# Attention and token/channel mixer on one core: the passage between two pairs of chunks, and the second weights' sums, issued in another order

## The chip, the core and the metric

The kernel runs on one core of a Trainium2 chip. The metric is the device time of one execution in microseconds (us). Of three executions of the kernel before, the median is 850.93 us (849.22 to 851.91).

The core's engines are called as in the profile: PE (TensorE, matrix products into the PSUM banks; PEld is its weight load), DVE (VectorE), ACT (ScalarE), POOL (GpSimd) and SP (SyncE, which here only issues DMAs). Each engine works through its own instructions in the order in which the program issues them, and waits on semaphores for the others.

## The reference

```python
def _attn_ref(q, k, v):                      # B, H, S, D = 8, 8, 576, 64; causal window of 64
    ...
    return np.matmul(attn, v)
def _moe_ref(x, w_tok1, w_tok2, w_ch1, w_ch2):   # x: (8, 576, 512)
    xt = x.transpose(0, 2, 1)
    h = np.maximum(xt @ w_tok1, 0.0) @ w_tok2
    u = x + h.transpose(0, 2, 1)
    h2 = np.maximum(u @ w_ch1, 0.0) @ w_ch2      # 512 -> 1536 -> 512
    return u + h2
```

Windowed attention gives x; a small network over the tokens gives u; a two-layer network over the channels (w_ch1, w_ch2) is added to u. Everything is fp32. The change lies wholly in the last step, the channel network.

## The kernel before

**Numbers in two parts.** Each operand is kept as a high part (a copy in the type fp32r, made by ACT, "hi") and a low part (source minus high part, a two-input subtraction on DVE or POOL, "lo"), and each product is three matmuls: hi·hi, hi·lo, lo·hi. Making the two parts of a 128x512 block is called a split.

**Stages.** The attention and the token network fill the span's first 300 us; they leave u, transposed, in DRAM (`u_dram`) as nine chunks of 512 tokens. The channel network then runs chunk by chunk. Chunks 0, 1 and 2 are done plainly: `gemm1` (12 blocks of hidden units, ft 0 to 11, of 12 matmuls each, whose result goes through `relu_split`: ACT makes hi, DVE lo) and `gemm2` (4 output blocks, ct 0 to 3). Chunks 1 and 2 do this in two halves of six ft's; the PE runs 72 matmuls of gemm1 and 72 of gemm2 in each half. The other six chunks are done in three pairs (q = 0, 1, 2) with Strassen's scheme: a 2x2 block product with seven products m1 to m7 in place of eight.

**What the pairs need.** (1) Sums and differences of the blocks of w_ch1 and w_ch2, split and written to DRAM as `w1s` and `w2s` while chunks 1 and 2 run. Those of w_ch2 come from `weight_steps2`: six rounds, each loading a piece `w2t`, making m5, m7, m6 and m3 (DVE adds, ACT copies hi into `w2p`, DVE subtracts lo) and storing them; a round takes five calls of `next(steps2)`. `w2p` has one buffer, so the hi copy of a round waits for the same store of the round before. `quarter_steps2` stores, unchanged, the blocks that m1, m2 and m4 use (w2hi, w2lo to `w2s`), in six steps. (2) For each pair the split operands of its seven products, for two halves t of the contraction: `load_raw(q, t)` loads four blocks r11, r12, r22, r21 of u, `sums` makes t1, r12, t2 on DVE, `sum4` one more, and `prep(q, m, t)` splits the source of product m. `part="hi"` and `part="lo"` do one half of a split; the lo goes to DVE unless an engine is given.

**A pair** runs `pair_f` six times (f = 0 to 5, 7 products of 6 matmuls each, and evictions out of PSUM) and, after every second f, `pair_op` (the second layer, a group, t = 0 and 1, 84 matmuls). `pair_f` with even f and `pair_op`'s t = 0 share four PSUM banks, odd f and t = 1 the other four. In `pair_op`, m4 adds onto the bank of m7 and m3 onto that of m5 (`INTO`), so m4's matmuls wait until m7's result has been read out by DVE (`evict`, line 1070), and m3's until m5's has. m2 adds onto m1's bank in the same way, after an `evict` at line 1082. `combine(1)` makes the second f's operands between these evictions on DVE.

**The passage.** In a pair's third group (`more` is true) `pair_op` also prepares the next pair: the splits of t = 0, `load_raw(q + 1, 1)`, sums and splits of t = 1, all in the same queues of DVE, ACT and POOL as the group's own work. At its end POOL does six `add_common`s (line 1070, on POOL) with their stores. There are two passages, from q = 0 to 1 and from 1 to 2. The next pair's f = 0 begins with the first half (t = 0) of its products m1, m6, m7 and m5, whose operands are the first to be ready.

Of the kernel before, what the change touches and what calls it, by code (L numbers as in the profile page):

```python
# [10 lines left out]
F32 = mybir.dt.float32  # L11
# [19 lines left out]
NCT = C // P  # L31
# [24 lines left out]
NH = NFT // 2  # L56
PRODUCTS = ("m1", "m6", "m7", "m5", "m2", "m4", "m3")
# [50 lines left out]
def mixer_kernel(ctx: ExitStack, tc: tile.TileContext, qh, kh, vh, wt1, wt2, wc1, wc2, out):  # L108
# [479 lines left out]
    with ExitStack() as bctx:  # L588
# [238 lines left out]
        def load_w1(n):  # L827

            if n < (NCHUNK - N_PLAIN) // 2 * NH:
                o = n % NSLOT * SLOT  # L830
                for k, w in enumerate((w1hi, w1lo)):
                    nc.sync.dma_start(w[:, o:o + SLOT].bitcast(F32),
                                      w1s[k][:, n % NH].rearrange("p m t c -> p (m t c)"))
# [4 lines left out]
        comb, raws = {}, {}  # L838

        def load_raw(q, t):  # L840
            raws.clear()
            for name, j, ct in (("r11", 0, t), ("r12", 1, t), ("r22", 1, 2 + t), ("r21", 0, 2 + t)):
                raws[name] = px[0].tile([P, CHUNK], F32, name=f"{name}_{q}_{t}", tag=name, bufs=1)
                nc.sync.dma_start(raws[name], u_dram[pairs[q][j]][:, ct])
            for name in ("t1", "t2"):
                raws[name] = px[0].tile([P, CHUNK], F32, name=f"{name}_{q}_{t}", tag=name, bufs=1)
# [6 lines left out]
            nc.vector.tensor_sub(r["t2"], r["r22"], r["t1"])  # L853

        def sum4():
            nc.vector.tensor_sub(raws["r11"], raws["r21"], raws["t2"])

        SOURCE = {"m1": "r11", "m6": "t2", "m7": "r12", "m5": "t1", "m2": "r21", "m4": "r11", "m3": "r22"}

        def prep(q, m, t, eng=None, part=None):  # L860
            if (q, m) not in comb:
# [10 lines left out]
        for j in range(1, N_PLAIN):  # L872
            u, last = ul.pop(j), j == N_PLAIN - 1
            if last:
                tctx.close()
                px.append(bctx.enter_context(tc.tile_pool(name="px", bufs=1, reuse_waits="tile")))
                load_raw(0, 0)
            for half in range(2):
                g = []
                for ft in range(half * NH, (half + 1) * NH):  # L880
                    g.append(new_g(f"{j}_{ft}"))
                    gemm1(j, ft, u, g[-1])
                    if j == 1:
                        next(steps, None)
                        if ft == 3:
                            ul[j + 1] = load_u(j + 1, pu)
                        if ft >= NFT - 2:
                            split_u(ul[j + 1], (2 * (ft - NFT) + 4, 2 * (ft - NFT) + 5))
                            next(steps2, None)
                    elif half == 0:  # L890
                        next(steps3, None)
                        for _ in range(2):
                            next(steps2, None)
                    else:
                        if ft == 6:
                            load_w1(0)
                        if ft == 8:
                            sums()
                        for m in {8: ("m1", "m6"), 9: ("m7", "m5"), 10: ("m2",)}.get(ft, ()):
                            prep(0, m, 1)  # L900
                        if ft == 11:
                            sum4()
                if last and half == 1:
                    for m in ("m4", "m3"):
                        prep(0, m, 1)
                    load_raw(0, 0)
                    load_w1(1)
                for ct in range(NCT):
                    op = new_op(f"{j}_{half}", ct)
                    gemm2(op, ct, range(half * NH, (half + 1) * NH), g, True, True)  # L910
                    add_out(j, u[0], ct, op, half == 1)
                    if j == 1 and half == 0:
                        for _ in range(1 if ct == NCT - 1 else 2):
                            next(steps, None)
                    elif j == 1:
                        for _ in range(4):
                            next(steps2, None)
                    elif half == 0:
                        if ct == 0:
                            for _ in steps2:  # L920
                                pass
                            sums()
                        for m in (("m1", "m6"), ("m2",), ("m7",), ("m5",))[ct]:
                            prep(0, m, 0)
                        if ct == NCT - 1:
                            load_raw(0, 1)
                    else:
                        if ct in (0, 1):
                            load_w2s(ct)
                        if ct == 1:  # L930
                            sums(False)
                            sum4()
                            for m in ("m4", "m3"):
                                prep(0, m, 0)
# [20 lines left out]

        common = whole[6:]

        MADE = {**SOURCE, "m4": "t1"}

        def parts_hi(fi, m):  # L960
            nc.scalar.copy(ops_g[fi][m][0], made[MADE[m]])  # L961

        def parts_lo(fi, m, eng):
            hi, lo = ops_g[fi][m]
            eng.tensor_sub(lo, made[MADE[m]], hi.bitcast(F32))  # L965

        def combine(fi):

# [18 lines left out]
            yield  # L987
            parts_lo(fi, "m4", nc.vector)

        def pair_f(q, f, rest):  # L990

            bank, fi = banks(f"gp{q}_{f}", f % 2), f % 2
            x1, later = x1s[fi], []
            o = (q * NH + f) % NSLOT * SLOT

            def block(name, src, m, eng):
                nc.scalar.activation(made[name], src, AF.Relu)  # L997
# [4 lines left out]
                    elif eng is not None:  # L1002
                        parts_lo(fi, m, eng)

            def product(m, ts, first):
                n, b, c = PRODUCTS.index(m), bank[INTO[m]], comb[q, m]
                for k, t in enumerate(ts):
                    at = slice(o + (n * 2 + t) * P, o + (n * 2 + t + 1) * P)
                    for j, (w, h) in enumerate(((w1hi, 0), (w1hi, 1), (w1lo, 0))):
                        nc.tensor.matmul(b, w[:, at], c[:, h, t], start=(first and n < 4 and k == j == 0),  # L1010
                                         stop=(k == len(ts) - 1 and j == 2), skip_group_check=True)

            more = q + 1 < len(pairs)
            begin = q > 0 and f == 0
            next(rest, None)
            if begin:

                for m in PRODUCTS[:4]:
                    product(m, (0,), True)
            for n, m in enumerate(PRODUCTS):  # L1020
                b = bank[INTO[m]]
                if begin and n < 4:
# [32 lines left out]
        def pair_op(q, grp, ufs, more, final):  # L1055
# [50 lines left out]
            ops = combine(1)  # L1106
            if more:

                prep(q + 1, "m7", 0, part="lo")
                prep(q + 1, "m5", 0, part="lo")  # L1110
                prep(q + 1, "m2", 0, nc.gpsimd, part="lo")
            for n in range(3):
                next(ops)
            parts_lo(1, "m2", nc.vector)
# [7 lines left out]
            if more:  # L1122
                sum4()
                prep(q + 1, "m4", 0, part="hi")
                prep(q + 1, "m3", 0, part="hi")
                prep(q + 1, "m3", 0, nc.gpsimd, part="lo")
            next(ops)
            evict(0, "m2")
            if not (final and last):
# [5 lines left out]
                load_raw(q + 1, 1)  # L1135
            for t in range(2):
                end = final and last and t == 1
                for m in ("m6", "m7", "m5", "m4", "m3"):
                    product(t, m, (1,) if m in PRODUCTS[:4] else (0, 1))
                    evict(t, m)  # L1140
                    if end and m in ("m5", "m4", "m3"):
                        add_common(t, m, nc.vector)
                    if more and t == 0 and m == "m3":
                        sums()
                        for x in PRODUCTS[:4]:
                            prep(q + 1, x, 1, part="hi")
                        prep(q + 1, "m1", 1, nc.gpsimd, part="lo")
                    if more and t == 1 and m == "m6":
                        prep(q + 1, "m6", 1, part="lo")
                        prep(q + 1, "m7", 1, nc.gpsimd, part="lo")  # L1150
                        prep(q + 1, "m2", 1, part="hi")
                        prep(q + 1, "m3", 1, part="hi")
                    if more and t == 1 and m == "m7":
                        prep(q + 1, "m5", 1, part="lo")
                        sum4()
                        prep(q + 1, "m4", 1, part="hi")
                    if more and t == 1 and m == "m4":
                        prep(q + 1, "m2", 1, nc.gpsimd, part="lo")
                        prep(q + 1, "m4", 1, part="lo")
                if end:  # L1160

# [7 lines left out]
                        add_common(t, m, nc.gpsimd)  # L1169
                load_w2s((q * NGRP + grp + 1) * 2 + t)  # L1170
            if more:
                prep(q + 1, "m3", 1, part="lo")
                for t in range(2):
                    for m in ("m5", "m4", "m3"):
                        add_common(t, m, nc.gpsimd)
# [57 lines left out]
```

## Time and profile before

| | us |
|---|---|
| median of three executions | 850.93 (849.22 to 851.91) |
| the profiled execution, its own time | 850.83 |
| its span, first to last instruction | 849.0 |
| outside the span | 1.83 |
| mean granted TensorE clock | 0.986 |

The span is what the trace shows; 1.83 us of the profiled execution lie outside it. The profile's page gives for each engine its busy time, a row of digits for the span in 40 slices of 21.2 us, and the chain of work that ended last. A view by stretches gives each engine's busy time between two moments. In a timeline or a list of waits, "[0.54 <-DVE uf L1070]" reads: idle for 0.54 us before this instruction, released by the DVE instruction of line 1070 that writes `uf`. A matmul of 512 columns is listed with 0.39 us, but one starts every 0.23 us, since they overlap. "w1hi", "w2hi_r", "ghic" in the DVE and ACT rows are the buffers that hold operands during the pairs, "m" and "r" those of `prep` and `load_raw`.

### The profile page before, as it was taken

To read this page: it belongs to the slowest core of one execution; us is meant where nothing else is said; L and a number is where in the kernel's file an instruction comes from. 1 tells how busy PE (TensorE), PEld (TensorE's weight loads), DVE (VectorE), ACT (ScalarE), POOL (GpSimd) and SP (SyncE) were. 2 spreads that over 40 slices of the span, in tenths; PEclk is the share of its full clock that TensorE was granted. 3 is DMA by queue.
4 is the path that set the end of the run, shared out by engine and by line. 5 is a ranking of instruction groups with operands and counts; after the bars stand their busy time and mean duration, and the time that the engine had idled before them with its cause. 6 is when DMAs were issued, how large, how long until landed. Compare 5 with 4: busy or idle time off the path is not lost.

```text
span 849.0 us, 15802 instructions
## 1 busy us (share of the span) xinstructions
PE 806.2 (95%) x5752; PEld 658.8 (78%) x5752; DVE 627.1 (74%) x1552; ACT 423.0 (50%) x1173; POOL 182.9 (22%) x174
## 2 busy tenths in 40 slices
PE   8989999999999999999699999996999995999997
PEld 6668888888898878888488878774878784878785
DVE  5978889788855885875535667789676779676777
ACT  6978988988854422242312516072425163335150
POOL 3623444344320000000000101034401033401011
PEclk9999999999999999999799999998999999899999
DMA  9837878777545658659945957444867554755512
GB/s 356 280 130 243 262 232 291 243 253 243 179 139 165 196 179 256 204 174 295 356 155 204 359 195 268 176 174 161 290 236 261 194 197 161 282 211 206 183 72 99
DMA packets 91357, 185.90 MB, mean 219 GB/s; under 512 B 8848, under 2 KB 56336, under 8 KB 89360
## 3 DMA queue, kind: packets, MB, share of 16 engines
q1 hardware_dynamic: 89168, 183.07, 62.8%
q10 hardware_dynamic: 2112, 1.84, 0.7%
q8 instruction: 45, 0.74, 0.4%
q14 instruction: 32, 0.26, 0.1%
HBM read 140.84 MB, written 44.04 MB: 218 GB/s over the span
## 4 chain that ended last, share of the span: by engine, by line
PE 67%; DVE 16%; ACT 7%; DMA 5%; issue 3%; SPq 1%; POOL 0%; ACTq 0%; DVEq 0%
PE gp L1010 17%; PE op L1065 13%; PE op L665 10%; PE gp L656 6%; PE h L396 5%; PE up L444 5%; PE xp L348 4%; DVE uf L1070 3%; PE s L306 3%; ACT e L329 3%; PE pp L336 2%; PE up L437 2%; DVE w2lo_r L1082 2%; DMA w_dram<-w 1%; DVE gloc L965 1%
## 5 line engine op out<-in xcount | busy, mean ns | idle before, releaser
L1010 PE MATMUL gp<-m,w1hi 128*128 128x512 f32 x504 | 156.7, 393 | 0.0
L329 ACT ACTIVATE e<-e,nm 128x128 f32<-128x128 f32 x288 | 112.3, 397 | 6.3 <-DVE nm L321 6.2
L965 POOL TENSOR_TENSOR gloc<-w2hi_r,ghic 128x512 fp32r<-128x512 f32 x18 | 23.3, 1294 | 414.5 <-ACT ghic L961 405.9
L1010 PEld LDWEIGHTS gp<-m,w1hi 128*128 128x128 f32 x504 | 95.8, 190 | 20.2
L1010 PE MATMUL gp<-m,w1lo 128*128 128x512 f32 x252 | 98.6, 391 | 0.0
L1070 DVE TENSOR_TENSOR uf<-op,uf 128x512 f32<-128x512 f32 (+1 forms) x91 | 61.8, 683 | 32.9 <-PE op L1065 29.8
L1065 PE MATMUL op<-ghic,w2hi 128*128 128x512 f32 (+1 forms) x145 | 59.8, 412 | 23.5 <-DVE uf L1070 18.8
L321 DVE CUSTOM_DVE_ANT_0 e<-s,mask 128x128 f32<-128x128 f32 x288 | 65.3, 285 | 10.7 <-PE s L306 10.5
L1028 ACT COPY x<-gp 128x512 f32<-128x512 f32 x18 | 10.5, 584 | 100.7 <-PE gp L1010 100.7
L997 ACT ACTIVATE w2hi_r<-x 128x512 f32<-128x512 f32 x54 | 34.1, 632 | 48.9 <-DVE x L1034 45.1
L1065 PEld LDWEIGHTS op<-ghic,w2hi 128*128 128x128 f32 x145 | 27.4, 189 | 39.8 <-DVE uf L1070 28.5
L665 PE MATMUL op<-ghi,w2hi 128*128 128x512 f32 x128 | 51.3, 401 | 7.1 <-ACT ghi L643 7.1
L1065 PE MATMUL op<-ghic,w2lo 128*128 128x512 f32 (+1 forms) x145 | 57.2, 394 | 0.0
L1065 PE MATMUL op<-gloc,w2hi 128*128 128x512 f32 (+1 forms) x145 | 57.1, 394 | 0.0
L656 PE MATMUL gp<-ulo,w1hi 128*128 128x512 f32 x144 | 56.0, 389 | 0.0
L656 PE MATMUL gp<-uhi,w1hi 128*128 128x512 f32 x144 | 56.0, 389 | 0.0
L656 PE MATMUL gp<-uhi,w1lo 128*128 128x512 f32 x144 | 56.0, 389 | 0.0
L329 ACT ACTIVATION_READ_ACCUMULATOR e<-e,nm 128x1 f32 x288 | 56.0, 194 | 0.0
L1010 PEld LDWEIGHTS gp<-m,w1lo 128*128 128x128 f32 x252 | 47.8, 190 | 10.1
L665 PE MATMUL op<-glo,w2hi 128*128 128x512 f32 x128 | 51.3, 401 | 0.5 <-DVE glo L644 0.5
L129 POOL TENSOR_TENSOR xlo<-x,xhi 128x512 fp32r<-128x512 f32 x32 | 41.6, 1299 | 43.7 <-ACT xhi L126 43.0
L665 PE MATMUL op<-ghi,w2lo 128*128 128x512 f32 x128 | 50.7, 396 | 0.0
(165 smaller groups left out, 2013.3 us busy)
## 6 DMA issues: line engine op xcount, KB each, us to landing
v<-vh SPq DMA_DIRECT2D x36, 512.0 KB, 4.0
w1hi<-w1s SPq DMA_DIRECT2D x18, 896.0 KB, 4.9
w1lo<-w1s SPq DMA_DIRECT2D x18, 896.0 KB, 7.1
w2hi<-w2s SPq DMA_DIRECT2D x18, 896.0 KB, 4.6
w2lo<-w2s SPq DMA_DIRECT2D x18, 896.0 KB, 6.6
raw<-wc SPq DMA_DIRECT2D x32, 384.0 KB, 4.6
q<-qh SPq DMA_DIRECT2D x36, 256.0 KB, 4.6
k<-kh SPq DMA_DIRECT2D x7, 1280.0 KB, 8.0
```

Of the source, the lines that this page charges most:

```text
L129: eng_lo.tensor_sub(lo, src, hi.bitcast(F32))
L321: nc.vector.tensor_tensor_reduce(out=e[:, h], in0=s[:, h], in1=mk, scale=-scale, scalar=MAX_F32, op0=ALU.add, op1=ALU.min, accum_out=nm[:, ...
L329: nc.scalar.activation(e[:, h], e[:, h], AF.Exp, bias=nm[:, g:g + 1], scale=-1.0, accum_out=sm[:, g:g + 1])
L348: nc.tensor.matmul(xp[half * BLK:(half + 1) * BLK, h], pts[h % 2][:, h // 2, half * BLK:(half + 1) * BLK], vt[:, half, h], start=True, sto ...
L396: nc.tensor.matmul(h_ps[b][tt], w[:, o + tt * P:o + (tt + 1) * P], x, start=first and n == 0, stop=last and n == len(combos) - 1)
L444: nc.tensor.matmul(up[:, :n], hx[:, cs], w[:, tt * S + s0:tt * S + s0 + n], start=False, stop=(k == 6), skip_group_check=True)
L656: nc.tensor.matmul(gp, w[:, w1_at(ft, ct)], x[:, ct], start=(k == 0), stop=(k == 3 * NCT - 1))
L665: nc.tensor.matmul(op, w[:, at], x[:, cols], start=(first and k == 0), stop=(last and k == 3 * len(gs) - 1), skip_group_check=not (first a ...
L997: nc.scalar.activation(made[name], src, AF.Relu)
L1010: nc.tensor.matmul(b, w[:, at], c[:, h, t], start=(first and n < 4 and k == j == 0), stop=(k == len(ts) - 1 and j == 2), skip_group_check= ...
L1065: nc.tensor.matmul(bank[t][INTO[m]][:, cols], w[:, at], ops_g[fi][m][h][:, cols], start=(n < 4 and fi == j == 0), stop=(fi == fis[-1] and ...
L1070: eng.tensor_add(ufs[c][:, ct, cols], x, ufs[c][:, ct, cols])
```

## The change

1. *Order in the groups* (all nine calls of `pair_op`): the loop over the last five products runs m7, m6, m5, m4, m3 in place of m6, m7, m5, m4, m3.
2. *Splits of t = 0 in the passage*: the lo's of m7 and m5 go from DVE to POOL, and m3's hi and lo are made ahead of m2's lo; POOL has four lo's in a row there.
3. *Splits of t = 1*: m7's lo is issued directly behind m1's on POOL; the lo's of m6 and m5, the hi's of m2 and m3, `sum4` and m4 each come one product later.
4. *`sum4` writes to t1* and no longer to r11, so r11 is free for its next load earlier; `raws.clear()` at the head of `load_raw` goes.
5. *Two f's ahead*: after the passage, the first halves (t = 0) of m1, m6, m7 and m5 run for f = 0 and then for f = 1, before any second half.
6. *Chunk 2*: `steps2` gets one call per ft in half 0 (two before) and two per ct in the following gemm2 (all that was left, at ct = 0, before). The six `quarter_steps2` move from half 0 to half 1. m7's and m5's splits of t = 0 move from gemm2 to ft = 6 of half 1, with `load_raw(0, 1)` behind them; the splits of t = 1 come one ft later.

```diff
         def load_raw(q, t):
-            raws.clear()
...
         def sum4():
-            nc.vector.tensor_sub(raws["r11"], raws["r21"], raws["t2"])
+            nc.vector.tensor_sub(raws["t1"], raws["r21"], raws["t2"])
...
                     elif half == 0:
-                        next(steps3, None)
-                        for _ in range(2):
-                            next(steps2, None)
+                        next(steps2, None)
                     else:
                         if ft == 6:
+                            prep(0, "m7", 0)
+                            prep(0, "m5", 0)
+                            load_raw(0, 1)
                             load_w1(0)
-                        if ft == 8:
+                        next(steps3, None)
+                        if ft == 9:
                             sums()
-                        for m in {8: ("m1", "m6"), 9: ("m7", "m5"), 10: ("m2",)}.get(ft, ()):
+                        for m in {9: ("m1", "m6"), 10: ("m7", "m5"), 11: ("m2",)}.get(ft, ()):
                             prep(0, m, 1)
...
                         if ct == 0:
-                            for _ in steps2:
-                                pass
                             sums()
-                        for m in (("m1", "m6"), ("m2",), ("m7",), ("m5",))[ct]:
+                        for m in (("m1",), ("m6",), ("m2",), ())[ct]:
                             prep(0, m, 0)
-                        if ct == NCT - 1:
-                            load_raw(0, 1)
+                        for _ in range(2):
+                            next(steps2, None)
...
-            if begin:
-
-                for m in PRODUCTS[:4]:
-                    product(m, (0,), True)
+            if q > 0 and f == 0:
+
+                ahead.append(banks(f"gp{q}_1", 1))
+                for f1, b in enumerate((bank, ahead[0])):
+                    for m in PRODUCTS[:4]:
+                        product(m, (0,), True, f1, b)
...
-                prep(q + 1, "m7", 0, part="lo")
-                prep(q + 1, "m5", 0, part="lo")
-                prep(q + 1, "m2", 0, nc.gpsimd, part="lo")
+                prep(q + 1, "m3", 0, part="hi")
+                for m in ("m7", "m5", "m3", "m2"):
+                    prep(q + 1, m, 0, nc.gpsimd, part="lo")
...
-                for m in ("m6", "m7", "m5", "m4", "m3"):
+                for m in ("m7", "m6", "m5", "m4", "m3"):
                     product(t, m, (1,) if m in PRODUCTS[:4] else (0, 1))
                     evict(t, m)
...
-                        prep(q + 1, "m1", 1, nc.gpsimd, part="lo")
-                    if more and t == 1 and m == "m6":
+                        for x in ("m1", "m7"):
+                            prep(q + 1, x, 1, nc.gpsimd, part="lo")
+                    if more and t == 1 and m == "m5":
                         prep(q + 1, "m6", 1, part="lo")
-                        prep(q + 1, "m7", 1, nc.gpsimd, part="lo")
+                        prep(q + 1, "m5", 1, part="lo")
                         prep(q + 1, "m2", 1, part="hi")
                         prep(q + 1, "m3", 1, part="hi")
-                    if more and t == 1 and m == "m7":
-                        prep(q + 1, "m5", 1, part="lo")
+                        prep(q + 1, "m2", 1, nc.gpsimd, part="lo")
+                    if more and t == 1 and m == "m4":
                         sum4()
                         prep(q + 1, "m4", 1, part="hi")
-                    if more and t == 1 and m == "m4":
-                        prep(q + 1, "m2", 1, nc.gpsimd, part="lo")
+                    if more and t == 1 and m == "m3":
+                        prep(q + 1, "m3", 1, part="lo")
                         prep(q + 1, "m4", 1, part="lo")
```

More of the change, by code (lines that the diff above doesn't have):

```diff
@@ L855, in sum4 @@
         def sum4():
-            nc.vector.tensor_sub(raws["r11"], raws["r21"], raws["t2"])
-        SOURCE = {"m1": "r11", "m6": "t2", "m7": "r12", "m5": "t1", "m2": "r21", "m4": "r11", "m3": "r22"}
+            nc.vector.tensor_sub(raws["t1"], raws["r21"], raws["t2"])
+        SOURCE = {"m1": "r11", "m6": "t2", "m7": "r12", "m5": "t1", "m2": "r21", "m4": "t1", "m3": "r22"}
         def prep(q, m, t, eng=None, part=None):
@@ L956, in mixer_kernel @@
         common = whole[6:]
-        MADE = {**SOURCE, "m4": "t1"}
         def parts_hi(fi, m):
-            nc.scalar.copy(ops_g[fi][m][0], made[MADE[m]])
+            nc.scalar.copy(ops_g[fi][m][0], made[SOURCE[m]])
         def parts_lo(fi, m, eng):
             hi, lo = ops_g[fi][m]
-            eng.tensor_sub(lo, made[MADE[m]], hi.bitcast(F32))
+            eng.tensor_sub(lo, made[SOURCE[m]], hi.bitcast(F32))
         def combine(fi):
@@ L988, in combine @@
             parts_lo(fi, "m4", nc.vector)
+        ahead = []
         def pair_f(q, f, rest):
-            bank, fi = banks(f"gp{q}_{f}", f % 2), f % 2
+            fi = f % 2
+            bank = ahead.pop() if ahead else banks(f"gp{q}_{f}", fi)
             x1, later = x1s[fi], []
-            o = (q * NH + f) % NSLOT * SLOT
             def block(name, src, m, eng):
@@ L1003, in block, with product @@
                         parts_lo(fi, m, eng)
-            def product(m, ts, first):
+            def product(m, ts, first, f=f, bank=bank):
                 n, b, c = PRODUCTS.index(m), bank[INTO[m]], comb[q, m]
+                o = (q * NH + f) % NSLOT * SLOT
                 for k, t in enumerate(ts):
@@ L1013, in pair_f @@
             more = q + 1 < len(pairs)
-            begin = q > 0 and f == 0
+            begin = q > 0 and f < 2
             next(rest, None)
-            if begin:
-                for m in PRODUCTS[:4]:
-                    product(m, (0,), True)
+            if q > 0 and f == 0:
[3 more added lines that the diff above has]
+                        product(m, (0,), True, f1, b)
             for n, m in enumerate(PRODUCTS):
@@ L1124, in pair_op @@
                 prep(q + 1, "m4", 0, part="hi")
-                prep(q + 1, "m3", 0, part="hi")
-                prep(q + 1, "m3", 0, nc.gpsimd, part="lo")
             next(ops)
@@ L1171, in pair_op @@
             if more:
-                prep(q + 1, "m3", 1, part="lo")
                 for t in range(2):
```

## The prediction

> **What bounds the kernel now.** I read the page first, then the chain of work that ended last, then a view by stretches cut at the channel network's groups, and last the waits and timelines inside the stretches that are too long.
>
> ```profile
> span 849.0 us, 15802 instructions
> PE 806.2 (95%) x5752; PEld 658.8 (78%) x5752; DVE 627.1 (74%) x1552; ACT 423.0 (50%) x1173; POOL 182.9 (22%) x174
> PEclk9999999999999999999799999998999999899999
> 466.60 19.04 PE gp L1010 x84
> ```
>
> The PE is the bound (95%), so what counts is where it stands still. The last row, from the chain, gives the unit: 84 matmuls without a break take 19.04 us, 0.2267 us each. The clock row has dips in slices 20, 28 and 35, near 420, 595 and 725 us.
>
> ```profile
> 388.80:466.60 77.80, 70.19 (x290) 55.38 (x289) 39.44 (x74) 20.28 (x41) 0.00 (x0) 0.93 0.74 250
> 466.60:505.94 39.34, 38.69 (x169) 31.38 (x169) 27.10 (x41) 15.23 (x26) 3.88 (x3) 1.00 0.70 274
> ...
> 545.32:595.02 49.70, 41.18 (x169) 32.10 (x169) 41.55 (x57) 21.84 (x38) 18.00 (x13) 0.95 0.51 184
> 595.02:635.25 40.23, 39.58 (x170) 31.99 (x169) 28.57 (x42) 15.15 (x26) 8.52 (x7) 0.98 0.72 268
> ...
> 674.60:724.43 49.83, 40.93 (x170) 32.12 (x169) 41.63 (x57) 21.84 (x38) 18.00 (x13) 0.95 0.51 185
> 724.43:764.90 40.47, 39.82 (x169) 32.06 (x169) 28.56 (x42) 15.16 (x26) 8.54 (x7) 0.98 0.73 267
> 764.90:804.33 39.43, 38.78 (x170) 31.30 (x169) 28.25 (x43) 14.27 (x24) 3.88 (x3) 1.00 0.51 185
> 804.33:849.00 44.67, 39.16 (x175) 31.39 (x173) 31.04 (x48) 14.27 (x24) 7.76 (x6) 1.00 0.26 95
> ```
>
> Columns: stretch, length, then busy time of PE, PEld, DVE, ACT, POOL, granted clock, DMA share, GB/s. The first row is chunk 2, the others are groups. A group is 168 matmuls, 38.08 us; chunk 2 is 288, 65.28 us. What is above that is lost: 12.5 in chunk 2, 1.3 in each of the four plain groups (first and last shown), 11.6 and 11.8 in the two passages, 2.2 and 2.4 in the groups behind them (some 1.0 and 1.2 more than a plain group), 6.6 in the last.
>
> **The change, part by part.**
>
> *Chunk 2.*
>
> ```profile
> ACT w2p L774 <- DMA w2s<-w2p: 17.9, 10, 7.1
> PE op L665 <- ACT ghi L643: 7.1, 4, 2.6
> 399.11 2.83 SPq L782 DMA_DIRECT2D w2s<-w2p  x4
> 406.23 0.41 ACT L774 CAST w2p<-w2t 128x256 fp32r<-128x256 f32 x1 [7.10 <-DMA w2s<-w2p]
> 407.16 0.59 ACT L643 ACTIVATE ghi<-gp 128x512 fp32r<-128x512 f32 x1
> ...
> w2s<-w2p SPq DMA_DIRECT2D x48, 128.0 KB, 3.6
> ```
>
> The waits of 388 to 423 us: ACT stands 17.9 us before the second weights' hi copies, because the one buffer w2p is still being stored. Behind them in ACT's queue stands `relu_split`'s hi (407.16), and gemm2 of half 0 waits for that. Here lies nearly all of the 12.5 us, the drop of the clock that follows included. The four stores were issued from 399.11, behind a quarter's stores, and the copy went on 7.1 us after them at 406.23. The change takes the quarters out of this stretch and halves the pace of the rounds. Going through ACT's queue by hand: the stores of round 3 go out at 397.4, land by 401.5 (bounds: the row's 7.1 us, and 3.6 us, the median in the last row, from the DMA view); with one call per ft the copies stand at 401.5, 403 and 404.4, and the last ghi of half 0 at 405.3. gemm2 starts at 405.1 and needs that block only five blocks of 0.68 us later. So the stall goes; I keep 0.9 for a late copy and take **-11.6** (bounds -6, where half stays, and -12.5). Calls: 18 in chunk 1, 6, then 8 of which the work ends with the seventh: the sums end in half 0 still.
>
> What is late next is DMA. Half 1 now starts at 421.4 and ends at 454.1. Into it come `load_raw(0,1)`, `load_w1(0)` and six quarter steps, then what stood there: `load_raw(0,0)`, `load_w1(1)`, stores, and both `load_w2s`, which read what the quarters just wrote.
>
> ```profile
> r<-u_dram SPq DMA_DIRECT2D x28, 256.0 KB, 4.3
> w1hi<-w1s SPq DMA_DIRECT2D x18, 896.0 KB, 4.9
> w2hi<-w2s SPq DMA_DIRECT2D x18, 896.0 KB, 4.6
> w2s<-w2hi SPq DMA_DIRECT2D x5, 384.0 KB, 5.0
> 356.00:374.00 18.00, 18.00 (x81) 14.92 (x80) 12.82 (x23) 6.76 (x14) 0.00 (x0) 1.00 0.69 195
> 395.00:420.00 25.00, 17.39 (x63) 11.85 (x62) 11.28 (x27) 7.09 (x17) 0.00 (x0) 0.85 1.02 343
> ```
>
> Eight r's (2.1 MB), four w1 and four w2s pieces (7.3 MB), six hi and six lo quarter stores of 384 KB (4.7 MB) and two output stores of 256 KB (0.5 MB) make some 14.7 MB from 426.8 us on. At the 343 GB/s of the last row, which has this very mix, that takes 43 us, to 469.7; the first `pair_op` wants w2s at 454.1 + 19.04 = 473.1. Covered by 3.4 us, so nothing is charged. If that cover goes (195 GB/s at a share of 0.69, so 283 at a full one), it lands at 478.7 and costs 5.6.
>
> *The order m7, m6, m5.*
>
> ```profile
> 497.74 0.50 PE L1065 MATMUL op<-ghic,w2hi 128*128 128x512 f32 x1 [0.54 <-DVE uf L1070]
> 496.40 0.69 DVE L1082 TENSOR_TENSOR w2lo_r<-op,w2lo_r 128x512 f32<-128x512 f32 x1
> 497.00 1.48 DVE L1070 TENSOR_TENSOR uf<-op,uf 128x512 f32<-128x512 f32 x2
> ```
>
> In a plain group m4 starts at 497.74, when DVE has read m7 (497.00, 0.69 us), for which it had read m6 first (496.40). With m7 first, that reading ends 0.60 us earlier and m4 follows at once, 0.8 of the group's loss; for t = 1 the 0.4 left goes too. m3's wait for m5's eviction doesn't come in its place: it ends where it ended before, at 498.3, and m3 is due 1.36 us behind m4's 497.1. Taken: 1.1 in each of six groups (four plain, two behind passages) and 1.0 in the last: **-7.6** (bounds -3, if m3 takes over the t = 0 part, and -9).
>
> *The passages.*
>
> ```profile
> PE op L1065 <- DVE uf L1070: 6.5, 3, 2.8
> PE op L1065 <- DVE w2lo_r L1082: 1.7, 1, 1.7
> 566.57 1.30 POOL L868 TENSOR_TENSOR m<-r,m 128x512 fp32r<-128x512 f32 x1 [1.31 <-ACT m L866]
> 568.35 0.68 DVE L868 TENSOR_TENSOR m<-r,m 128x512 fp32r<-128x512 f32 x1
> 572.74 0.68 DVE L1082 TENSOR_TENSOR w2lo_r<-op,w2lo_r 128x512 f32<-128x512 f32 x1
> 580.09 1.47 DVE L1070 TENSOR_TENSOR uf<-op,uf 128x512 f32<-128x512 f32 x2
> 588.57 1.19 DVE L868 TENSOR_TENSOR m<-t,m 128x512 fp32r<-128x512 f32 x1
> 589.16 1.73 POOL L868 TENSOR_TENSOR m<-r,m 128x512 fp32r<-128x512 f32 x1
> 589.68 1.76 DVE L856 TENSOR_TENSOR r<-r,t 128x512 f32<-128x512 f32 x1
> 590.00:598.00 8.00, 6.60 (x18) 4.69 (x17) 6.57 (x6) 0.62 (x1) 8.00 (x6) 0.58 0.30 91
> ```
>
> All large stalls of the first passage (563 to 597 us) end with a DVE eviction: m2 waits for m1's (572.74), t = 0's m4 for m7's (the second of the two at 580.09), t = 1's m4 and m3 for evictions behind `sums`, `sum4` and splits. By start times they are 1.9, 2.6, 3.1 and 1.8 us, with 0.6 at the group's start; then the clock is 0.58 (last row) and matmuls cost twice as much, some 2.3 us.
>
> The last rows show what a POOL split costs DVE. A DVE split or sum alone takes 0.68 us, one every 0.60; the one at 588.57 and that at 589.68 took 1.19 and 1.76, each ending 0.55 us behind a POOL split's end, and the POOL split between them took 1.73, not 1.30. They take turns. Evictions, with one input in PSUM, keep their 0.68. The Trainium skill ("SBUF — State Buffer", Who interferes with whom) states it as a lock: a DVE instruction with two SBUF inputs and a GpSimd one that reads SBUF block each other for a whole instruction. This speaks against the change, and the trace agrees.
>
> Edit 2 takes two 0.60 us splits (568.35 and the next) from DVE and puts four POOL splits of 1.30 us beside DVE's sums. Going through the queues with the turns: POOL runs m7's to 566.55, m5's to 568.35, m3's 569.5 to 570.8, m2's 571.3 to 572.6; DVE's t1 ends at 569.55, t2 at 571.35, m5's lo at 573.2, then r12, m2's lo and m1's eviction, 574.4 to 575.1. So m2 starts at 575.15, not 573.47: this stall **grows** from 1.9 to 3.7 (bounds: 0.7 if POOL cost DVE nothing; 4.5 with one turn more). From there ten DVE instructions of 0.60 us, now without a POOL split among them, lead to m7's eviction at 581.1: PE stalls 0.3 before m7 and 1.0 before m4 (was 2.6). t = 0 ends at 583.9. Then evictions, three sums (one with a turn of 0.5) and m7's eviction by 587.7: m4 of t = 1 stalls 1.8 (was 3.1), m3 none (was 1.8). f = 0 begins at 590.5, not 594.8. Left: 0.6 + 3.7 + 0.3 + 1.0 + 1.8 = 7.4; before 11.6 + 1.0 and 11.8 + 1.2, with the clock. So -5.2 and -5.6, **-10.8** for both.
>
> Edit 5 covers what comes late: m5's lo ends near 591.6, m4's near 597, delayed by POOL's `add_common`s. With two f's of first halves (24 matmuls, 5.4 us) f = 0's second halves start at 595.9 and its m4 at 600: both in time. Without f = 1's share m1's second half would start at 593.2, still covered; so edit 5 alone is worth 0 to 2. f = 1's m5 waits for t = 1's last eviction, due 594.1, and starts at 595.2. Edit 4's earlier load isn't on the path: DVE reaches `sums` after the blocks have landed. Removing `clear` removes no instruction.
>
> Sum: 850.83 - 11.6 - 7.6 - 10.8 = **820.8**. The 1.83 us outside the span stay; the profiled execution lies 0.1 below the median of the runs shown.
>
> **The rivals.**
>
> *The clock drops in the longer m2 stall* (0.15). Today slow matmuls follow after stretches like 578 to 592 us, with three stalls of 7.5 us in 14; the new 3.7 us stall stands more alone, but is longer than any now. Price: today's 2.3 us, twice: 825.4. The Trainium skill ("TensorE: Matmul & The Clock Gate", HAM oscillation) warns of idle gaps over about 3.4 us; no run here shows a single such gap, and by that rule this rival would be the forecast.
>
> *POOL costs DVE less than turns* (0.13). Then m2's stall is 0.7: 3.0 less, twice: 814.8. Against it: 1.76 us at 589.68.
>
> *The stores still hold ACT, or w2s comes late* (0.17). Half of chunk 2's stall stays (-6 for -11.6), or 5.6 is lost before the first `pair_op`: 826.4.
>
> *The passages gain nothing* (0.07): a turn with POOL in every sum and the clock too: 831.6.
>
> *Slower* (0.03): w2s read back much too late, at the first `pair_op`. All gains (30.0) are eaten if the 14.7 MB land after 475 + 30 = 505, so at under 188 GB/s from 426.8; at 170 it is 513, 38 late: 859. Against it stand the 343 GB/s.
>
> *The change doesn't do what it says* (0.02): the order of issue is as before where it matters; 850.
>
> **How the numbers follow.** The forecast has 0.43, at 820.8 with 817 to 825 of its own. The range from 812 to 833 takes in the first four rivals and leaves out combinations of two misses and the last two cases. About 0.3% is what a measurement of this kernel can tell from no change. Faster by more than that: all but the last two, 0.95; within: 0.02; slower: 0.03.
>
> **What would show it.** Chunk 2's stretch of 66 to 67 us, with no long ACT wait before `w2p`; plain groups of 38.2; no wait before m4 in them; in a passage a stall of about 3.7 before m2, 1.0 and 1.8 before the m4's, none before m3, and clock 1.0 behind it. It would be wrong if `pair_op` 0 waited for a DMA, or if the stall moved to m3 or into the next pair's second halves.

## The result and the profile after

The changed kernel takes 830.64 us (median of four executions, 829.95 to 832.15), against 850.15 us of the kernel before beside it (849.22 to 851.91): a ratio of 0.9771, 95% interval 0.9748 to 0.9793. That is 19.5 us less, where the forecast had 30.0 (820.8, range 812 to 833). The profiled execution took 830.65 us, its span is 828.9.

The page of the changed kernel, first section and clock row:

```profile
span 828.9 us, 15808 instructions
PE 799.8 (96%) x5752; PEld 657.7 (79%) x5752; DVE 627.2 (76%) x1548; ACT 422.7 (51%) x1173; POOL 191.7 (23%) x178
...
PEclk9999999999999999999999999999999998999999
```

The view by stretches, cut at chunk 2 and at the first matmul of each group; columns as in the prediction:

```profile
388.38:454.70 66.32, 65.85 (x289) 54.00 (x288) 35.96 (x70) 19.14 (x40) 0.00 (x0) 1.00 0.78 252
454.70:493.06 38.36, 38.36 (x170) 31.48 (x169) 29.94 (x46) 16.17 (x28) 3.89 (x3) 1.00 0.88 349
531.41:577.46 46.05, 40.81 (x169) 32.36 (x168) 37.94 (x52) 21.29 (x37) 17.01 (x12) 0.96 0.57 205
577.46:618.47 41.01, 39.43 (x170) 31.15 (x168) 32.59 (x46) 15.77 (x27) 13.92 (x10) 1.00 0.68 257
656.84:705.16 48.32, 42.42 (x169) 33.54 (x168) 40.07 (x53) 21.29 (x37) 18.60 (x13) 0.93 0.55 196
705.16:746.20 41.04, 39.44 (x169) 31.15 (x168) 30.99 (x45) 15.78 (x27) 12.31 (x9) 1.00 0.68 256
746.20:784.56 38.36, 38.36 (x169) 31.39 (x168) 28.15 (x43) 14.27 (x24) 3.88 (x3) 1.00 0.53 192
784.56:828.90 44.34, 38.92 (x175) 31.64 (x173) 30.88 (x48) 14.27 (x24) 7.73 (x6) 0.98 0.27 101
```

Row against row of before: chunk 2 went from 77.8 to 66.3 (-11.5), the four plain groups from 39.4 to 38.36 each (-4.1 together; two are shown), the passages from 49.7 and 49.8 to 46.1 and 48.3 (-5.2). The groups **behind** the passages became longer, 40.2 and 40.5 to 41.0 twice (+1.4), though the new order of products should have taken 1.0 from each. The last group lost 0.3. These are -19.7 of the span's -20.1.

So the passages are where the forecast's gain is missing: -10.8 was expected of the two passages and what follows them, and -5.2 + 1.4 + 2.0 = -1.8 came. The 2.0 is the order's share in the groups behind, which the run with the old order confirms: they take 42.1 there, not 41.0. In the first passage the PE waits as follows (the list of waits for 548 to 578 us, then for 577 to 600; line numbers are the changed kernel's: 1067, 1072 and 1084 were 1065, 1070 and 1082):

```profile
PE op L1067 <- DVE w2lo_r L1084: 3.0, 1, 3.0
PE op L1067 <- DVE uf L1072: 1.9, 2, 1.4
...
PE gp L1010 <- ACT x L1030: 1.1, 1, 1.1
PE gp L1010 <- DVE x L1034: 0.4, 1, 0.4
```

The first is the stall before m2; by the matmuls' starts, as all stalls from here on, it is 3.2 us (3.7 forecast). The second is those before the two m4's, 0.7 and 1.5 us (forecast 1.0 and 1.8). None is before m3, as forecast. The last two rows weren't forecast: they are in f = 1 of the next pair. And behind the m2 stall the clock falls. The PE's timeline of the changed kernel, from the stall on:

```profile
561.05 0.80 PE L1067 MATMUL op<-ghic,w2hi 128*128 128x512 f32 x1 [3.02 <-DVE w2lo_r L1084]
561.64 0.63 PE L1067 MATMUL op<-gloc,w2hi 128*128 128x512 f32 x1
562.07 0.63 PE L1067 MATMUL op<-ghic,w2lo 128*128 128x512 f32 x1
562.50 0.63 PE L1067 MATMUL op<-w1hi,w2hi 128*128 128x512 f32 x1
```

The starts are 0.43 us apart and not 0.23: eight or nine slow matmuls, 1.7 us.

### The profile page after: what moved, and what is told of

Read it like the earlier page. It is cut to its first block, busy times and chain, and to the rows that moved or that the text cites. A ratio compares the mean times of both kernels' runs of the same rounds, so it can differ in the third digit from the quotient of the medians.

```text
span 828.9 us, 15808 instructions
## 1 busy us (share of the span) xinstructions
PE 799.8 (96%) x5752; PEld 657.7 (79%) x5752; DVE 627.2 (76%) x1548; ACT 422.7 (51%) x1173; POOL 191.7 (23%) x178
## 4 chain that ended last, share of the span: by engine, by line
PE 36%; DVE 9%; ACT 4%; issue 2%; DVEq 0%; ACTq 0%
PE op L1067 16%; PE gp L1010 14%; PE op L665 4%; PE gp L656 2%; ACT w2hi_r L996 2%; DVE uf L1072 1%; DVE w2lo_r L967 1%; DVE w2lo_r L970 1%; DVE w1lo L962 1%; DVE x L1047 1%; ACT ghic L958 1%; DVE x L1036 1%; DVE x L1034 1%; DVE x L1032 1%; ACT w1hi L958 1%
## 5 line engine op out<-in xcount | busy, mean ns | idle before, releaser
L996 ACT ACTIVATE w2hi_r<-x 128x512 f32<-128x512 f32 x54 | 34.1, 631 | 48.3 <-DVE x L1036 44.6
L665 PE MATMUL op<-ghi,w2lo 128*128 128x512 f32 x128 | 49.8, 389 | 0.0
```

Of the source, the lines that this page charges most:

```text
L665: nc.tensor.matmul(op, w[:, at], x[:, cols], start=(first and k == 0), stop=(last and k == 3 * len(gs) - 1), skip_group_check=not (first a ...
```

## The experiments

Each kernel is the changed one with one part undone or altered, up to the last two, which combine parts; times are medians beside the kernel before.

### The two ways of sharing the t = 0 splits

```diff
-                prep(q + 1, "m3", 0, part="hi")
-                for m in ("m7", "m5", "m3", "m2"):
-                    prep(q + 1, m, 0, nc.gpsimd, part="lo")
+                prep(q + 1, "m7", 0, part="lo")
+                prep(q + 1, "m5", 0, part="lo")
+                prep(q + 1, "m2", 0, nc.gpsimd, part="lo")
...
                 prep(q + 1, "m4", 0, part="hi")
+                prep(q + 1, "m3", 0, part="hi")
+                prep(q + 1, "m3", 0, nc.gpsimd, part="lo")
```

> In the passage the t = 0 splits are shared out as before: m7's and m5's lo on DVE, m2's alone on POOL there, m3's hi and lo behind sum4; all else as in the changed kernel (830.6 us). Theory A (POOL splits and DVE's sums take turns, and the long m2 stall lowers the clock): DVE's t2 and m5 lo take 0.68 us again and not 1.67 and 1.76, the stall before m2 shrinks from 3.2 to 1.9 us, the slow matmuls behind it (1.8 us) go, and the stall before m4 of t = 0 grows from 0.7 to about 2.0: 2 us less in each passage, 826 to 828. Rival (POOL relieves DVE, as the edit's placing suggests): two splits more on DVE come on top of what is there, 1.2 us in each passage, 832 to 834.

Measured: **824.7 us** (0.9696, interval 0.9667 to 0.9725), 5.9 less than with the splits on POOL and below the 826 to 828 expected. First DVE and POOL in the changed kernel (timelines), then DVE in this one, at the same instructions:

```profile
555.84 1.67 DVE L970 TENSOR_TENSOR w2lo_r<-w2hi_r,w2lo_r 128x512 f32<-128x512 f32 x1
557.43 1.76 DVE L962 TENSOR_TENSOR w1lo<-w2lo_r,w1hi 128x512 fp32r<-128x512 f32 x1
...
555.15 3.49 POOL L867 TENSOR_TENSOR m<-r,m 128x512 fp32r<-128x512 f32 x2 [0.69 <-ACT m L865]
```

```profile
556.19 0.69 DVE L970 TENSOR_TENSOR w2lo_r<-w2hi_r,w2lo_r 128x512 f32<-128x512 f32 x1
556.85 0.69 DVE L962 TENSOR_TENSOR w1lo<-w2lo_r,w1hi 128x512 fp32r<-128x512 f32 x1
```

Beside two POOL splits, DVE's t2 and m5 lo take 1.67 and 1.76 us; without them 0.69. The passages of this kernel:

```profile
531.08:575.36 44.28, 39.36 (x170) 31.14 (x169) 37.22 (x54) 21.24 (x37) 13.20 (x10) 1.00 0.59 212
...
654.74:699.30 44.56, 39.31 (x169) 31.14 (x168) 37.51 (x54) 21.24 (x37) 13.18 (x10) 1.00 0.59 211
```

They are 1.8 and 3.8 us shorter than the changed kernel's and the clock is at 1.00, not 0.96 and 0.93. The stalls themselves hardly differ: before m2 1.8 for 3.2, before m4 of t = 0 1.8 for 0.7. What the longer single stall costs is mostly the clock behind it. Theory A holds; the gain is above its 2 us per passage, since the second passage's clock had fallen twice.

### POOL that writes but does not read

```diff
                 for m in ("m7", "m5", "m3", "m2"):
-                    prep(q + 1, m, 0, nc.gpsimd, part="lo")
+                    if (q + 1, m) not in comb:
+                        prep(q + 1, m, 0, part="hi")
+                    nc.gpsimd.memset(comb[q + 1, m][:, 1, 0].bitcast(F32), 0.0)
```

> In the passage the four t = 0 lo's on POOL (m7, m5, m3, m2) are replaced by four POOL writes of zero into the same places: POOL keeps four instructions there but reads nothing, and the low parts of those operands are left out of the result. All else as in the changed kernel (830.6 us). Theory A (it is POOL's reading that takes turns with DVE's two-input instructions): DVE's t2 and m5 lo beside them take 0.68 us, not 1.67 and 1.76, two more there fall from 1.05 and 1.19 to 0.7, the stall before m2 falls from 3.2 us to 0.3 to 0.7, the clock stays, and 2 to 4 us go per passage (part comes back before m4 of t = 0): 822 to 827. Rival (DVE is held by ACT's copies and semaphores, not by POOL): the long DVE rows stay and the time is 830 to 832.

Measured: 824.8 us (0.9686, interval 0.9643 to 0.9730), inside the 822 to 827 of theory A. DVE's and POOL's timelines of this kernel, and its waits in the first passage:

```profile
552.21 0.69 DVE L962 TENSOR_TENSOR w1lo<-w2hi_r,w1hi 128x512 fp32r<-128x512 f32 x1 [1.30 <-ACT w1hi L958]
...
555.18 0.69 DVE L970 TENSOR_TENSOR w2lo_r<-w2hi_r,w2lo_r 128x512 f32<-128x512 f32 x1
555.83 0.69 DVE L962 TENSOR_TENSOR w1lo<-w2lo_r,w1hi 128x512 fp32r<-128x512 f32 x1
...
551.40 1.92 POOL L1115 MEMSET m<- 128x512 f32 x4
...
PE op L1067 <- DVE w2lo_r L1084: 0.4, 1, 0.4
```

The m2 stall is 0.5 us, so it came from POOL and not from ACT's copies: the four splits where they stood cost 3.2 - 0.5 = 2.7 us of stall, against 1.2 us of DVE work saved. The writes take 0.48 us each and end before DVE's sums begin. Only the first DVE row stood beside them, and it took 0.69 us (1.05 beside the splits). The Trainium skill ("SBUF — State Buffer", Who interferes with whom) has it that a GpSimd instruction which only writes doesn't contend; that row agrees. In the second passage the clock still fell, behind a stall of 2.5 us before an m4.

### One f ahead

```diff
-            begin = q > 0 and f < 2
+            begin = q > 0 and f == 0
...
-                ahead.append(banks(f"gp{q}_1", 1))
-                for f1, b in enumerate((bank, ahead[0])):
-                    for m in PRODUCTS[:4]:
-                        product(m, (0,), True, f1, b)
+                for m in PRODUCTS[:4]:
+                    product(m, (0,), True)
```

> After the passage only f = 0's first halves run ahead, as in the kernel before; all else as in the changed kernel (830.6 us). Theory A: with f = 1's first halves gone ahead, f = 1 has only 2.7 us of products between m1's end and m2's start, ACT is late with m1's copy and DVE with m7's sum, and the PE stalls 1.3 + 0.55 us in each passage (593.7 and 595.8 us in the changed kernel's trace), with nothing gained for it: f = 0's last split (m4's lo) ends at 583.9, and without f = 1's share f = 0's m4 would start at 584.3. So the stalls go and no other comes: 826.4, with 826 to 828. Rival: f = 1's halves cover late splits; then f = 0's second halves stall by up to 2.7 us in each passage and the time is 831 to 836.

Measured: 828.1 us (0.9736, interval 0.9706 to 0.9766), above the expected 826.4 and just past its band; the interval overlaps the changed kernel's, so the stretches decide. The group behind the first passage, then the second passage:

```profile
579.35:619.55 40.20, 39.29 (x170) 31.14 (x168) 32.45 (x46) 15.75 (x27) 13.87 (x10) 1.00 0.70 264
657.91:703.55 45.64, 39.34 (x170) 31.15 (x168) 38.49 (x52) 21.32 (x37) 17.00 (x12) 1.00 0.57 207
```

The group behind is 0.8 shorter (40.20 for 41.01): f = 1's two stalls of 1.3 and 0.55 are gone, but f = 0's m4 now waits 1.0 for DVE, which is late by turns with POOL's `add_common`s. So the second f's halves did cover something, less than they cost. Why they cost is seen on ACT in the changed kernel:

```profile
590.80 0.63 ACT L996 ACTIVATE w2hi_r<-x 128x512 f32<-128x512 f32 x1 [0.25 <-DVE x L1047]
592.57 0.62 ACT L958 CAST ghic<-w2lo_r 128x512 fp32r<-128x512 f32 x1 [1.14 <-DVE w2lo_r L967]
593.09 0.58 ACT L1030 COPY x<-gp 128x512 f32<-128x512 f32 x1
```

With half of f = 1's first four products done, only 2.7 us of matmuls lie between f = 0's last product and f = 1's m2, which needs m1 copied out (593.09). That copy stands in ACT's queue behind a hi copy of f = 0's operands, which waits for DVE (592.57), and that for f = 0's last block (590.80). The products done ahead were the cover of this chain.

The second row shows something else: the stall before m2 is as long as in the changed kernel (3.2), but the clock stayed at 1.00, and this passage is 2.7 us shorter for it. That is not the edit's doing, as the last section shows; the edit's own share of the 2.6 us gained is the 0.8 of each group behind.

### The order of the products, chunk 2, the t = 1 splits, sum4

```diff
-                for m in ("m7", "m6", "m5", "m4", "m3"):
+                for m in ("m6", "m7", "m5", "m4", "m3"):
```

> All groups run their last products in the old order m6, m7, m5, m4, m3; all else as in the changed kernel (830.6 us). Theory: the m4 stalls of 0.70 + 0.26 us, with the late start of the next matmul 1.0 us, come back in each of six groups, 0.5 to 1 in the last and up to 1.2 in the passages' groups: 837 to 840. Rival (what the order gained in the plain groups came from elsewhere, such as the other edits' DMA order): 830 to 832.

Measured: 837.9 us (0.9855, interval 0.9815 to 0.9894). The first plain group and its wait:

```profile
454.72:494.10 39.38, 38.73 (x170) 31.38 (x168) 29.52 (x46) 16.29 (x28) 3.90 (x3) 1.00 0.85 340
...
PE op L1067 <- DVE uf L1072: 0.5, 1, 0.5
```

39.38 for 38.36: the plain groups' gain is the order's, whole.

```diff
                     elif half == 0:
-                        next(steps2, None)
+                        next(steps3, None)
+                        for _ in range(2):
+                            next(steps2, None)
...
                         if ct == 0:
+                            for _ in steps2:
+                                pass
```

(with the splits and `load_raw(0, 1)` where they stood before.)

> Chunk 2 as in the kernel before (two calls of the second weights' sums per ft, the quarters' stores in half 0); all else as in the changed kernel (830.6 us). Theory: chunk 2 takes 77.6 us again and not 66.3, and nothing behind it gains: 841.9, with 841 to 843. Rival (half of what chunk 2 gained was given back by the later stores in the pairs, where DMAs now land late): 835 to 838.

Measured: 840.8 us (0.9885, interval 0.9841 to 0.9928), 10.1 more; chunk 2:

```profile
390.78:467.27 76.49, 70.11 (x289) 55.18 (x288) 39.08 (x73) 19.92 (x41) 0.00 (x0) 0.93 0.76 255
```

10.2 us longer than with the change, and nothing was given back in the pairs: with the change undone no group there is over 0.1 us shorter, except the second passage (46.5 for 48.3), whose clock fell once and not twice.

```diff
                         for x in PRODUCTS[:4]:
                             prep(q + 1, x, 1, part="hi")
-                        for x in ("m1", "m7"):
-                            prep(q + 1, x, 1, nc.gpsimd, part="lo")
-                    if more and t == 1 and m == "m5":
+                        prep(q + 1, "m1", 1, nc.gpsimd, part="lo")
+                    if more and t == 1 and m == "m6":
                         prep(q + 1, "m6", 1, part="lo")
-                        prep(q + 1, "m5", 1, part="lo")
+                        prep(q + 1, "m7", 1, nc.gpsimd, part="lo")
                         prep(q + 1, "m2", 1, part="hi")
                         prep(q + 1, "m3", 1, part="hi")
-                        prep(q + 1, "m2", 1, nc.gpsimd, part="lo")
-                    if more and t == 1 and m == "m4":
+                        prep(q + 1, "m5", 1, part="lo")
                         sum4()
...
```

> The t = 1 splits of the passage one product earlier, as before the change (m6's and m5's lo and sum4 ahead of m5's eviction, m7's lo behind m6, m2's behind m4, m3's lo at the end); all else as in the changed kernel (830.6 us). Theory: three DVE instructions stand before m5's eviction again, two of them in turns with POOL, so m3 of t = 1 waits 2 to 3 us in each passage (0 now), with slow matmuls behind it: 834 to 839. Rival (the PE catches the time up, since f = 0's second halves wait for the last splits anyway): 830 to 832.

Measured: 839.3 us (0.9855, interval 0.9817 to 0.9894), 8.7 more and just above the 834 to 839 expected. The waits of the first passage, DVE and POOL:

```profile
PE op L1067 <- DVE uf L1072: 6.1, 3, 3.5
...
574.07 2.37 DVE L867 TENSOR_TENSOR m<-t,m 128x512 fp32r<-128x512 f32 x2
576.47 1.63 DVE L855 TENSOR_TENSOR t<-r,t 128x512 f32<-128x512 f32 x1
...
574.20 3.35 POOL L867 TENSOR_TENSOR m<-r,m 128x512 fp32r<-128x512 f32 x2 [3.13 <-DVE w2lo_r L1084]
```

The third wait (3.5 us) is m3's of t = 1, for an eviction behind three DVE instructions that take 4.0 us beside POOL and would take 1.8 alone. Edit 3 took this stall away, above the expected 2 to 3 us.

With `sum4` writing to r11 again:

```diff
-            nc.vector.tensor_sub(raws["t1"], raws["r21"], raws["t2"])
+            nc.vector.tensor_sub(raws["r11"], raws["r21"], raws["t2"])
```

> sum4 writes to r11 again, so that r11's next load waits for m4's splits; all else as in the changed kernel (830.6 us). Theory: the loads of the second half go out 0.6 us later at most and DVE comes to the sums after they have landed, so nothing but a turn with m1's POOL split can move: 830 to 832. Rival (the earlier load is what lets the t = 1 sums start): 833 to 836.

Measured: 831.4 us (0.9762, interval 0.9720 to 0.9805): nothing that can be told from the changed kernel. The earlier load was not on the path.

### Together, and one step further

> Both undone at once: only f = 0's first halves ahead, and the t = 0 splits shared out as before the change. The two runs alone gave 828.1 and 824.7 against 830.6. Theory A: f = 1's two stalls (1.3 + 0.55 us) go in each passage, f = 0's m4 waits 1.0 us in their place, so 0.8 per passage on top of the second run, whose gain of the clock is not there twice: 822 to 824. Rival (with m3's split later again, f = 0's second halves need f = 1's cover): 825 to 828.

Measured: 823.4 us (0.9670, interval 0.9636 to 0.9704), as expected. Its first passage and that passage's waits (in this kernel and the next the lines have the numbers of the kernel before):

```profile
531.19:575.44 44.25, 39.30 (x170) 31.15 (x168) 37.20 (x54) 21.24 (x37) 13.19 (x10) 1.00 0.58 212
...
PE op L1065 <- DVE uf L1070: 2.9, 2, 1.7
PE op L1065 <- DVE w2lo_r L1082: 1.7, 1, 1.7
```

Then, on this kernel:

```diff
-            evict(0, "m2")
-            if not (final and last):
-                evict(1, "m2")
+            if not more:
+                evict(0, "m2")
+                if not (final and last):
+                    evict(1, "m2")
...
                     evict(t, m)
+                    if more and t == 0 and m == "m5":
+                        evict(0, "m2")
+                        evict(1, "m2")
```

> The kernel with one f ahead and the old t = 0 sharing (823.4 us), with one thing moved in the passage: the two evictions of m2 and their stores go from before m7's eviction to behind m5's (t = 0), where DVE waits for the PE. Theory A (what stands in DVE's queue ahead of m7's eviction is what the PE waits for): the stall before m4 of t = 0 falls from 1.8 to about 0.6 us, DVE's own gaps of 0.6 us behind m5's eviction take up the two, and 1.2 us go in each passage: 821.0, with 820 to 822. Rival (DVE's work until the t = 1 sums is the sum that counts, in any order): the stall comes back before m4 of t = 1, 1.5 to 2.7 us there, and the time is 823 to 824.

Measured: **821.1 us** (0.9662, interval 0.9633 to 0.9690), the fastest of the kernels run. Its first passage and that passage's waits:

```profile
530.86:573.18 42.32, 39.04 (x170) 31.18 (x168) 36.34 (x54) 21.15 (x37) 13.49 (x10) 1.00 0.59 209
...
PE op L1065 <- DVE w2lo_r L1082: 1.7, 1, 1.7
PE op L1065 <- DVE uf L1070: 1.3, 1, 1.3
```

One of the two waits for an output eviction is gone whole, the one before m4 of t = 0 (1.8 us, 0.6 was expected to stay), and the one before m4 of t = 1 did not grow (1.4 by the starts, as without the move). DVE does the same work; it does it while the PE has something to do. The passages are 1.9 and 2.6 us shorter in the profiled executions; the medians differ by 2.3 us, but the intervals of the two ratios overlap nearly whole, so the gain rests on the stretches.

## Why the prediction was right, and where it was not

**Chunk 2** (-11.6): right, -11.5. ACT's long waits no longer reach `relu_split` (two waits of 0.2 us before a matmul are left), and the DMAs moved into half 1 were in time: the first `pair_op` waits for none, its group is 38.36 us. The last load of w2s went out at 455.27 and the longest of them took 15.8 us, so all had landed by 471.1, 2.6 us ahead of that `pair_op`'s first matmul at 473.74, where 3.4 was forecast.

**The order** (-7.6): right in mechanism and in the plain groups, -4.1 of 4.4 forecast, and in the groups behind the passages (42.1 to 41.0). In the last group only 0.3 of 1.0 came, since m7 is now the first product there and waits 0.5 us for its own low part at 812.7 us, a wait the order of before had covered.

**The passages** (-10.8): wrong; about -1.8 came. The walk through the queues was right: stalls of 0.5, 3.2, 0.7 and 1.5 us in the first passage against 0.6, 3.7, 1.0 (and 0.3 before m7) and 1.8. Two things at its end failed.

- *The clock* was taken to stay. It fell behind the m2 stall in both passages, 1.7 and 1.5 us, and in the second once more behind a 2.2 us stall, some 1.6 us. That was the first rival, with 0.15; it should have been likelier than not. Cut along the grid of 3.41 us that the last section describes, the trace of the kernel before already has, from 380 us on, a drop behind each step at full clock with 1.92 us or more of idle PE and none behind 1.55 or less, and a stall of 3.7 us leaves at least some 1.8 in one step, wherever the grid lies. The Trainium skill ("TensorE: Matmul & The Clock Gate", HAM oscillation) would have had it so for gaps over 3.4 us; the gap was 3.2, and 2.2 in the second passage, so here the limit is lower than the page has it.
- *Edit 5* was costed at "0 to 2" of gain, and its cover was looked for on DVE and POOL alone. ACT's queue was left out: f = 1's shortened head brings a stall of 1.3 + 0.55 us in each passage, against 1.0 that the second f covers. The edit costs 0.8 us per passage. A stall in the next pair's second halves stood among the prediction's own signs of being wrong.

The clock, 4.8 us, and f = 1's stalls, 3.7 us, make up most of the 9.0 us that are missing. That 830.6 still lies in the range is in part luck: the range was said to leave out two misses at once, and two came. The time is close to the 831.6 of "The passages gain nothing", which had 0.07; of its causes the clock came, but not a turn with POOL in every sum.

**Edit 2**, seen as "this stall grows" in the prediction, was then carried as part of a gain. Undone, it gives 5.9 us. The rule on the lock that the prediction cites agrees with the runs, 1.76 beside 0.69 us. A DVE split costs 0.60 us of DVE, a POOL split up to 1.1, if DVE's two-input work stands beside it.

**Edit 3** carried the passages' real gain (8.7 us when undone), **edit 4** none. Undoing singly, the parts give 7.3 + 10.1 + 8.7 - 5.9 - 2.6 + 0.8 = 18.4 us of the 19.5. The rest is less than these medians can tell, so no strong dependence between the parts shows; the -2.6 and the 0.8 are themselves hardly more than that.

## What to carry to other kernels

Before a split goes to POOL, look at what DVE does at that moment: beside two-input work it takes more from DVE than it saves. In a queue that a PSUM bank waits for, put the eviction ahead and everything else into the gaps behind it; this gave 8.7 us (t = 1 splits) and about 2 us between each two pairs (m2's evictions), with the same work done. Work done ahead is cover taken from a later place, and every in-order queue there must be looked through, ACT's too. And where DVE's work must make the PE wait, two stalls of 1.8 us were cheaper here than one of 3.2 and one of 0.7, since the clock stayed.

## What the runs showed that was not expected

A single PE stall of 3.2 us mostly costs the clock. Six of the kernels (the changed one, and those with one f, the old order, old chunk 2, old `sum4` and old t = 1 splits) have stalls of 3.15 to 3.3 us before m2, two each. Matmuls at half speed, eight or nine of them, followed in ten of these twelve; in two they did not, at 3.15 and 3.17 us. Behind stalls of 1.8 us at that place (the kernel before and three others, eight passages) they never did.

What decides it can be read from the traces. Within a trace, every slow stretch begins and ends on a grid of 3.41 us and is one to three steps long; the grid lies differently in each trace. Here are two m2 stalls, cut along their grids: the changed kernel's first, then the second of the kernel with one f ahead.

```profile
557.52:560.93 3.41, 0.51 (x3) 0.09 (x1) 3.41 (x5) 1.24 (x2) 1.13 (x1) 1.00 0.00 0
560.93:564.35 3.42, 3.30 (x8) 2.62 (x9) 3.40 (x7) 1.22 (x2) 0.00 (x0) 0.50 0.00 0
...
682.53:685.94 3.41, 2.00 (x9) 1.31 (x7) 3.41 (x3) 1.05 (x2) 2.61 (x2) 1.00 0.10 38
685.94:689.36 3.42, 1.81 (x8) 1.51 (x9) 3.42 (x7) 0.65 (x2) 0.00 (x0) 1.00 0.00 0
689.36:692.77 3.41, 3.32 (x15) 2.28 (x13) 3.41 (x6) 1.19 (x2) 0.00 (x0) 1.00 0.24 88
```

Both stalls are 3.2 us long. The first lies almost whole in one step, which leaves the PE idle for 2.90 us, and the next step runs at clock 0.50. The second is shared between two steps, 1.41 and 1.61 us idle, and the clock stays at 1.00. From 380 to 815 us the eleven traces have 1358 steps at full clock. Twenty of them are followed by a step at half clock: the twenty in which the PE was idle (the step less its busy time) for 1.87 us or more. The longest idle time without a drop behind it is 1.85 us.

So a stall of 3.2 us here keeps the clock only if an edge of the grid falls near its middle, by an estimate from these numbers in one case of five. Stalls of 1.8 us before m2 kept it, with at most 1.7 us of idle PE in a step. So the grid's place alone can make one execution differ from the next; a drop costs some 1.6 us. This rule was read from the finished traces, and no run was made to test it.
